# Three row broadcasts: a matmul with a matrix of ones replaced by a write to DRAM and a broadcast read on GpSimd's queue

## The chip, the cores and the metric

The kernel runs on one core of a Trainium2 chip. The metric is device microseconds of one execution of the whole program; the figure given for the kernel before is the median of three runs.

A core has TensorE (PE in the profile, with its weight loads as PEld), VectorE (DVE), ScalarE (ACT), GpSimd (POOL) and SyncE (SP). SP, ACT and POOL also issue DMAs; "SPq", "ACTq" and "POOLq" are these engines as issuers.

## What is computed

One transformer block with adaptive layer norm, batch 1, 2048 tokens, width D = 1024, in bf16:

```python
mod = (silu(c) @ w_mod).reshape(1, 6, 1, 1024)      # c: (1, 1024), w_mod: (1024, 6144)
sa, ca, ga, sb, cb, gb = mod[:, 0], ..., mod[:, 5]
h = layernorm(x) * (1 + ca) + sa
x = x + ga * attention(h)          # 32 query heads on 4 cached kv heads, the last 512 keys, then @ wo
h = layernorm(x) * (1 + cb) + sb
x = x + gb * (silu(h @ w_gate) * (h @ w_up) @ w_down)   # inner width 3584
```

Three vectors of 1024 elements are needed as rows that are the same on all 128 partitions: the gates `ga` and `gb`, which multiply outputs that lie with tokens on the partitions, and `silu(c)`, the conditioning row. That one is multiplied with transposed slices of `w_mod` on VectorE to make the last 24 columns of `mod`.

## The kernel before, in words

All operations are recorded through a tracker, `T.op(stream, emit, reads, writes)` (L80), which puts semaphore waits ahead of an instruction on its engine from the buffers that it reads and writes. Instructions run on each engine in the order in which the program records them; a wait holds all that stands behind it on the same engine. DMAs recorded with a stream of GpSimd are issued by GpSimd in its own instruction order.

The program has an opening (loads, statistics, the first projections), attention on the first 1024 tokens (iterations i = 0 to 65 of `attend`, with `pre0` and `tick0`), the output projection `o_phase(0)`, attention on the second 1024 tokens (i = 64 to 129, with `pre1` and `tick1`), `o_phase(1)`, and the feed-forward part. Large products use a seven-product scheme on 2 x 2 blocks, so sums of weight blocks have to be prepared ahead of their use.

One iteration of `attend` handles one head on 512 tokens: `pre(i)`, part of a query projection, the scores of iteration i - 1 (L797, four matmuls of 512 columns into PSUM banks 0 to 3, then two exponentials on ACT at L805 over two banks each), the products with v for iteration i - 2 (L808: reciprocal at L824, normalisation at L827 on VectorE, and a DMA transpose at L830 on SP), the rest of a query projection, and `tick(i)`. In the first 24 iterations queries are projected whole (`qproj`, copied out of PSUM at L656); later in seven products with sums at L835 and L906.

Beside attention runs the preparation of weight sums for `wo` and `w_down` in units of 512 KB (`unit_chain`, L962). `unit_load` (L945) issues a load on GpSimd's queue into one of two slots, `unit_sums` makes four sums on VectorE (L956) and issues a store on GpSimd's queue (L960). The load for the unit after the next one goes into the slot just stored, so GpSimd waits for the store to land before it issues it.

The conditioning: `silu(c)` lies as `sc_bf`, element k * 128 + p on partition p, column k. The columns of `mod` come out the same way, in `mod_bf`. `ga` is made by matmuls in iterations 12 to 14; the last 24 columns by `mod_col` (L603) on VectorE, one every fourth iteration from i = 19 to 111, each a multiplication of a transposed slice of `w_mod` with `sc_row`, summed along the row. After the last, `mod_take` (L608) copies them to `mod_bf`.

To turn such a [128, 8] block into a row on all partitions, `row_task` (L612) does this: ACT copies the block to f32 (L613); for each of two halves ACT makes four matrices of 128 x 128, each the identity scaled per partition by one column (L618); PE multiplies a matrix of ones with them, which puts the four columns as 512 row elements on every partition in PSUM bank 7 (`XB`); VectorE copies that bank to the row (L626). Matmuls all have line L272 in the profile.

`row_task` is a generator. It is put into the list `bgx` at three places: in `pre0(5)` for `sc_row`, in `pre0(14)` for `rowb[0]` (`ga`), and in `mods(111)` for `rowb[1]` (`gb`). `run_x`, called in `tick0` and `tick1`, moves it on by one step. A row task therefore takes three calls. `rowb[0]` is first read in `o_phase(0)`, `rowb[1]` in the feed-forward part.

GpSimd otherwise does small work: a few fills at the start, among them `ones_bf`, and for each tile of tokens two operations that make the reciprocal standard deviation (L418 and L420 in `aggr`, L535 and L536 in `rstd_of`).

The softmax here doesn't subtract the row's maximum and nothing guards it: scores larger than these inputs give would overflow.

## Time and profile before

| | |
|---|---|
| median of 3 runs | 1160.29 us (1160.15 to 1160.33) |
| profiled execution, time | 1160.09 us |
| profiled execution, span of the core | 1158.3 us |
| granted TensorE clock | full speed throughout |
| PE busy | 1148.3 us |
| DVE busy | 817.4 us |
| ACT busy | 532.7 us |
| POOL busy | 68.4 us |
| DMA | 179.98 MB, 155 GB/s over the span |
| row tasks run at | 45 to 52 us, 78 to 86 us, 500 to 528 us |

How to read it: the span runs from the first to the last instruction of the program; the execution's time is a little longer. In a list of groups, a line gives source line, engine, operation, out<-in by tile names (`arena` is one large SBUF tensor that holds most tiles, `ps` is PSUM), partitions x elements and type, count, then busy time, mean ns of one instruction, and the idle time of the engine just before such instructions with what ended it. In a timeline, a line gives start and length in microseconds, and in brackets the idle time before it and what released it. The chain of waits is followed backwards from the last instruction: at each step to what released it, or to the instruction before it on the same engine. Matmuls are pipelined, so the length of one says less than the distance to the start of the next.

### The profile page before, as it was taken

Reading aid. Unit: us, or ns where it says so; the run is one execution under the profiler, and the core shown is the slowest. Engines: PE = TensorE matmul, PEld = TensorE weight load, DVE = VectorE, ACT = ScalarE, POOL = GpSimd, SP = SyncE. Lnnn points to the kernel's source line nnn. Section 1 sums busy time; section 2 is a strip of 40 time slices with the busy share of each in tenths; the row PEclk is TensorE's granted clock in tenths of the full one; section 3 lists DMA queues with packets and bytes.
Section 4 is the critical chain, followed back from the end, with each engine's and each line's share of the span. In section 5 each row is a group of like instructions: output and inputs, shape, how many; then the busy total and the mean of one; then the engine's idle time right before and its main releaser. Section 6 shows DMA issues by size and latency. Waiting matters only on the chain.

```text
span 1158.3 us, 18250 instructions
## 1 busy us (share of the span) xinstructions
PE 1148.3 (99%) x7105; PEld 588.0 (51%) x7105; DVE 817.4 (71%) x1638; ACT 532.7 (46%) x745; POOL 68.4 (6%) x137
## 2 busy tenths in 40 slices
PE   8999999999999999999999999999999999999999
PEld 5565556654445666656444444444444444444444
DVE  4858897757567777686567898777558777776536
ACT  3867777731127777787110354454110444544110
POOL 1100221100000111111000010000000000000000
PEclk9999999999999999999999999999999999999999
DMA  9679999976807898844875332323774424234443
GB/s 330 145 181 207 225 217 211 236 182 194 242 3 183 197 194 204 203 94 119 191 198 165 87 95 73 108 75 100 209 201 143 121 73 109 73 98 131 130 160 109
DMA packets 289941, 179.98 MB, mean 155 GB/s; under 512 B 130496, under 2 KB 278080, under 8 KB 289856
## 3 DMA queue, kind: packets, MB, share of 16 engines
q1 hardware_dynamic: 226880, 92.31, 35.5%
q10 hardware_dynamic: 54336, 55.05, 15.0%
q0 software_dynamic: 8640, 31.46, 9.3%
q8 instruction: 56, 0.92, 0.3%
q14 instruction: 29, 0.24, 0.1%
HBM read 128.45 MB, written 19.92 MB: 128 GB/s over the span
## 4 chain that ended last, share of the span: by engine, by line
PE 96%; DVE 2%; ACT 1%; DMA 1%; issue 0%; SPq 0%; ACTq 0%; DVEq 0%
PE ps L272 96%; ACT arena L805 1%; DMA arena<-in_A_wq_dram 1%; DVE arena L835 1%; DVE arena L906 0%; DVE st L413 0%; SPq L341 0%; SPq L310 0%; PE ps L276 0%; ACT arena L618 0%; DVE arena L852 0%; ACT tmp L743 0%; DVE arena L1566 0%; ACT L1551 0%; DVE arena L827 0%
## 5 line engine op out<-in xcount | busy, mean ns | idle before, releaser
L272 PE MATMUL ps<-arena 128*128 128x512 f16 (+2 forms) x6800 | 1141.2, 330 | 7.0 <-POOL arena L406 2.2
L272 PEld LDWEIGHTS ps<-arena 128*128 128x128 bf16 (+1 forms) x6800 | 577.8, 98 | 563.0 <-DVE arena L835 6.2
L805 ACT ACTIVATE arena<-ps 128x1024 bf16<-128x1024 f32 x256 | 261.5, 1022 | 44.6 <-PE ps L272 32.8
L838 ACT ACTIVATE tmp<-ps 128x512 f32<-128x512 f32 x167 | 99.7, 597 | 295.9 <-PE ps L272 280.8
L906 DVE TENSOR_TENSOR arena<-arena 128x512 f16<-128x512 bf16 x328 | 133.3, 419 | 3.0
L835 DVE TENSOR_TENSOR arena<-ps,tmp 128x512 bf16<-128x512 f32 (+1 forms) x134 | 91.8, 685 | 49.3 <-PE ps L272 37.8
L838 ACT ACTIVATE nsc<-ps 128x512 f32<-128x512 f32 x84 | 50.1, 596 | 93.2 <-PE ps L272 90.9
L827 DVE TENSOR_TENSOR arena<-ps,rl 128x512 f16<-128x512 f32 x128 | 88.5, 691 | 4.9 <-DVE rl L824 0.5
L835 DVE TENSOR_TENSOR arena<-ps,nsc 128x512 f16<-128x512 f32 x84 | 57.3, 687 | 41.2 <-PE ps L272 30.0
L824 DVE RECIPROCAL rl<-ps 128x4 f32<-128x4 f32 x128 | 23.1, 180 | 87.1 <-PE ps L272 86.2
L1551 ACT ACTIVATE arena<-arena 128x512 f16<-128x512 f16 x84 | 49.9, 624 | 32.4 <-DVE arena L835 32.4
L1122 DVE TENSOR_TENSOR tmp<-ps,tmp 128x512 f32<-128x512 f32 x32 | 22.1, 690 | 58.5 <-ACT tmp L838 48.8
L1046 DVE TENSOR_TENSOR arena<-arena 128x2048 f16<-128x2048 f16 (+3 forms) x56 | 56.0, 1010 | 9.3 <-PE ps L272 8.8
L838 ACT ACTIVATE arena<-ps 128x512 f32<-128x512 f32 x16 | 9.6, 597 | 90.5 <-PE ps L272 90.5
L956 DVE TENSOR_TENSOR arena<-arena 128x512 f16<-128x512 bf16 x120 | 47.9, 419 | 2.0 <-DMA arena<-in_A_wo_dram 0.9
L413 DVE BATCH_NORM_STATS2 st<-x_res 128x6 f32<-128x512 bf16 x58 | 39.5, 682 | 3.7 <-DMA x_res<-in_A_x_dram 3.5
L1566 DVE TENSOR_TENSOR arena<-arena 128x512 f16<-128x512 f16 x84 | 35.0, 416 | 0.3
L1123 DVE TENSOR_TENSOR tmp<-tmp,rowb 128x512 f32<-128x512 f32 (+1 forms) x49 | 33.7, 687 | 1.7
L427 DVE TENSOR_SCALAR nsc<-x_res,mv,rstd 128x1024 f16<-128x1024 bf16 (+1 forms) x30 | 16.2, 539 | 23.3 <-DMA arena<-nsc 22.4
L603 DVE SCALAR_TENSOR_TENSOR arena<-arena 128x1024 bf16<-128x1024 bf16 x24 | 29.2, 1215 | 0.0
L1124 DVE TENSOR_TENSOR arena<-tmp,x_res 128x512 bf16<-128x512 f32 (+1 forms) x33 | 22.3, 676 | 1.1
L835 DVE TENSOR_TENSOR arena<-ps,rowb 128x512 f16<-128x512 f32 x28 | 19.3, 690 | 3.9 <-ACT rowb L838 3.4
(87 smaller groups left out, 333.4 us busy)
## 6 DMA issues: line engine op xcount, KB each, us to landing
arena<-in_A_wq_dram SPq DMA_DIRECT2D x28, 512.0 KB, 5.3
arena<-wo_sum ACTq DMA_DIRECT2D x7, 2048.0 KB, 8.6
arena<-in_B_w_gate_dram SPq DMA_DIRECT2D x28, 512.0 KB, 4.0
arena<-in_B_w_up_dram SPq DMA_DIRECT2D x28, 512.0 KB, 5.1
arena<-wd_sum ACTq DMA_DIRECT2D x8, 1792.0 KB, 7.8
arena<-in_B_w_down_dram ACTq DMA_DIRECT2D x6, 1792.0 KB, 7.1
arena<-in_A_wo_dram POOLq DMA_DIRECT2D x16, 512.0 KB, 4.8
wo_sum<-arena POOLq DMA_DIRECT2D x16, 512.0 KB, 4.6
```

Source lines behind the costliest of these rows:

```text
L272: T.op(PE, lambda: TE.matmul(out_ap, lhsT, rhs, start=start, stop=stop, skip_group_check=skip), reads=reads, writes=[bank_buf])
L413: T.op(DVE, lambda: V.bn_stats(st_[sl][:, hf * 6:hf * 6 + 6], x_res[:, t, hf * 512:hf * 512 + 512]), reads=[B_x[t]], writes=[B_st[sl]])
L805: T.op(ACT, lambda: A.activation(ex_s[es][:, 2 * kp:2 * kp + 2, :], banks2(SCB + 2 * kp), AF.Exp, scale=att_scale), writes=[PB[SCB + 2 * k ...
L827: T.op(DVE, lambda: V.tensor_tensor(o_s[os_].rearrange("p (a b) d -> p a b d", a=2), psap(PVB * 512, [[512, 2], [130, 2], [1, P]]), rlb, A ...
L835: T.op(DVE, lambda: V.tensor_tensor(out, bank(ba), other, ADD), reads=[ob2], writes=[PB[ba], ob])
L838: T.op(ACT, lambda: A.activation(dst, bank(bk), AF.Copy), writes=[PB[bk], db])
L906: T.op(st, lambda: eng.tensor_tensor(o, a, b, op), reads=rd, writes=[wr])
L956: T.op(DVE, lambda: V.tensor_tensor(o, a, b, SUB), reads=rd, writes=[wr])
L1046: T.op(DVE, lambda: V.tensor_tensor(o, a, b, SUB), reads=rd, writes=[sb])
L1123: T.op(DVE, lambda: V.tensor_tensor(tm, tm, rw, MULT), reads=[B_row[row]], writes=[tb])
L1551: T.op(ACT, lambda: A.activation(o, s_, AF.Silu), reads=[sb], writes=[ob])
L1566: T.op(DVE, lambda: V.tensor_tensor(gu[blk][:, p, :], o, s_, MULT), reads=[sb, ob], writes=[B_gu[blk][p]])
```

## The change

`row_task`, its buffers (`c6`, `ones_bf`, the four `diag` matrices), the list `bgx` and all calls of `run_x` go. In their place `row_of` issues two DMAs from GpSimd's queue at the three places where a row task had been put into the list: the first writes the [128, 8] block into a DRAM tensor of 1024 elements in row order, the second, which waits for the first to land, reads that row to all 128 partitions with a step of zero.

```diff
-            T.op(POOL, lambda: g.memset(ones_bf, 1.0), writes=[B_ones])
...
-            def row_task(dst, dbuf, src, sbuf):
-                T.op(ACT, lambda: A.activation(c6[:, :], src, AF.Copy), reads=[sbuf], writes=[B_c6])
...
-                for n in range(2):
-                    for q in range(4):
-                        mm(bank(XB, P, q * P), ones_bf, diag[q], q == 0, q == 3, [B_ones, B_diag[q]], PB[XB], skip=True)
-                    T.op(DVE, lambda: V.tensor_copy(dst[:, n * 512:(n + 1) * 512], bank(XB)),
-                         writes=[PB[XB], dbuf])
-                    if n == 0:
-                        diags(1)
-                    yield
+            Q_row = [[dq("q_row%d_%d" % (n, m), nc.gpsimd) for m in range(2)] for n in range(3)]
+            rows_d = [nc.dram_tensor("row%d" % n, [D], BF16).ap() for n in range(3)]
+
+            def row_of(n, dst, dbuf, src, sbuf):
+                b_ = _Buf("rowd%d" % n)
+                T.op(Q_row[n][0], lambda: g.dma_start(rows_d[n].rearrange("(k p) -> p k", p=P), src, allow_slow_non_contiguous=True), reads=[sbuf], writes=[b_])
+                every = bass.AP(tensor=rows_d[n].tensor, offset=0, ap=[[0, P], [1, D]])
+                T.op(Q_row[n][1], lambda: g.dma_start(dst, every), reads=[b_], writes=[dbuf])
...
-                            bgx.append(row_task(rowb[1], B_row[1], mod_bf[:, 5 * DT:6 * DT], B_late[3]))
+                            row_of(1, rowb[1][:, :], B_row[1], mod_bf[:, 5 * DT:6 * DT], B_late[3])
...
-                    bgx.append(row_task(sc_row, B_scr, sc_bf[:, :], B_sc))
+                    row_of(2, sc_row, B_scr, sc_bf[:, :], B_sc)
...
-                        bgx.append(row_task(rowb[0], B_row[0], mod_bf[:, NE:NF], B_late[0]))
+                        row_of(0, rowb[0][:, :], B_row[0], mod_bf[:, NE:NF], B_late[0])
...
-                if i < 20 or i % 4 == 0:
-                    run_x()
```

## The prediction

> **What bounds the kernel now.** I read the busy shares first, then the chain that ended last, then the PE waits, and only then the surroundings of the three row tasks. The page:

> ```profile
> PE 1148.3 (99%) x7105; PEld 588.0 (51%) x7105; DVE 817.4 (71%) x1638; ACT 532.7 (46%) x745; POOL 68.4 (6%) x137
> PE 96%; DVE 2%; ACT 1%; DMA 1%; issue 0%; SPq 0%; ACTq 0%; DVEq 0%
> ```

> TensorE is the bound: it is busy 99% of the span and holds 96% of the chain. So a matmul removed is worth its streaming time, and ACT, VectorE or GpSimd work is worth something only where PE waits for it. After the first 16 us the list of waits has few entries (waited for, total, times, longest):

> ```profile
> PE ps L272 <- ACT arena L805: 1.4, 4, 0.5
> PE ps L272 <- DVE arena L835: 1.1, 3, 0.4
> PE ps L272 <- DVE arena L432: 0.5, 1, 0.5
> ```

> L805 is the exponential. The chain restricted to 40 to 120 us shows that some of its 1.4 us belong to the first row task (start, length, engine, tile, line):

> ```profile
> 44.14 1.02 ACT arena L805
> 45.16 0.11 ACT c L613
> 45.27 0.02 issue
> 45.29 1.28 ACT arena L618 x4
> 46.57 0.92 ACT arena L805
> ...
> 48.65 5.25 PE ps L272 x50
> ```

> L613 and L618 are the row task's scaled-identity copies. They stand between two exponentials on ACT, and PE stands behind the second. From the starts of single matmuls in the trace, PE's next score matmul starts at 47.53, 0.41 us later than back to back, and the third at 48.65, 0.67 us later. The copies of the second and third row (78 to 83 us; 500 and 514 us) are followed by no PE gap.

> The row matmuls themselves, by form (count, busy, mean ns, idle before):

> ```profile
> L272 PE MATMUL ps<-arena 128*128 128x128 bf16 x24 | 2.3, 219 | 0.0
> ```

> 219 ns is a pipelined duration; what one costs PE is the distance between starts, 56 ns in the trace.

> [...]here it makes 1024 writes of 2 bytes per row, 64 on each of 16 engines. [...] The trace shows such waits on this queue, 3.55 us for a store below.

> **Part by part.** All times are against the profiled execution, 1160.09 us (span 1158.3 and 1.8 around it), 0.20 under the median 1160.29.

> *PE work removed.* 24 matmuls x 56 ns = 1.34 us. Second row: 8 x 56 = 0.45 us, PE being gapless there. Third row: 0.45 likewise.

> *First row (sc_row), PE and ACT together.* Without the copies the exponential waits only for PE's two score matmuls, which end near 45.75 instead of ACT starting at 46.48. Two halves of 1.06 follow, so PE's third score matmul can start at 47.93 instead of 48.65: 0.72 gained (the first four row matmuls lay inside that stall). The four later ones add 4 x 56 = 0.22. Sum 0.94. The later stall behind L432 stays: VectorE was idle 0.33 us for PE just before it, so both move together.

> *VectorE.* Six PSUM copies of 0.68 us go (4.1 us). In none of their places does PE wait for VectorE in the next microseconds, so I count nothing. If the cover were gone it would be a gain, at most the 1.1 + 0.5 us above.

> *GpSimd memset of the ones.* 0.20 us at 1.42 us; PE's start is later held by weights landing (0.85 us idle at 11.58). Nothing; bounds 0 and -0.2.

> Gross gain 0.94 + 0.45 + 0.45 = 1.84 us.

> *What is added: six DMAs in GpSimd's order.* GpSimd issues the write, waits for its landing, issues the broadcast read; everything behind it in program order waits too. The consumers of the rows are far away: sc_row is first multiplied at 94 us, the gate rows after 260 us. So only the queue behind counts.

> First row (sc_row), near 44 us: GpSimd is then idle 11.09 us, until two unit loads at 55.13. Free up to some 9 us of write. Its packets share engines with the last norm transposes (landing 48.15), needed at 51.62, nearer 50.1 once VectorE is relieved; 0 to 1 us, I take 0.

> Third row, 497 us: behind it wait a pair of rstd operations (499.15, no reader for tens of microseconds) and the last store (501.73). Free.

> Second row, 76 us, is where it matters. GpSimd around it:

> ```profile
> 79.61 0.71 POOL L945 DMA_DIRECT2D arena<-in_A_wo_dram  x1 [3.55 <-DMA wo_sum<-arena]
> 87.20 0.57 POOL L960 DMA_DIRECT2D wo_sum<-arena  x1 [6.87 <-DVE arena L956]
> 92.53 0.71 POOL L945 DMA_DIRECT2D arena<-in_A_wo_dram  x1 [4.76 <-DMA wo_sum<-arena]
> ```

> The write is issued at 80.32, right behind a 512 KB load on the same queue; that load lands at 87.37. The queue works in order: two loads issued 0.95 us apart at 55.13 land 3.6 us apart. So the write lands at 87.37 + w. Size of w: the profile's queue table gives 35.5% x 16 x 1158.3 / 226880 = 29 ns per packet of 407 B and 51 ns per packet of 1013 B, which extrapolates to 14 ns at no size, 64 x 14 = 0.9 us. [...] I take 30 ns: w = 1.9, landing 89.3. Issuing the read (0.7) moves the store from 87.20 to 90.0. The store landed 4.8 after issue; the 256 KB read ahead of it adds 128 packets / 16 x 0.09 = 0.7. So the load of 92.53 goes out at 95.5, three late. It landed at 98.07 and was first read at 100.09, 2.0 us of slack; with PE 0.45 further ahead VectorE then waits 3.0 + 0.45 - 2.0 = 1.45 us. What VectorE has to give:

> ```profile
> 100.09 0.88 DVE L956 TENSOR_TENSOR arena<-arena 128x512 f16<-128x512 bf16 x2
> 101.34 0.18 DVE L824 RECIPROCAL rl<-ps 128x4 f32<-128x4 f32 x1 [0.37 <-PE ps L272]
> ...
> 103.97 0.18 DVE L824 RECIPROCAL rl<-ps 128x4 f32<-128x4 f32 x1 [0.26 <-PE ps L272]
> ```

> 0.37 + 0.26 = 0.63 us of idleness, then it runs solid until PE already waits for it at 110.7. So PE loses 1.45 - 0.63 = 0.8 us. Each further microsecond of w is a further microsecond lost.

> The issue of 1024 descriptors on GpSimd itself: the 0.57 of a store with 128 rows against 0.71 of a load with 256 source rows gives about 1 ns per descriptor, 1.5 us in all, hidden behind the load that is still moving. At three times that it would still end before 87.37.

> Sum: 1160.09 - 1.84 + 0.8 = 1159.05; on the scale of the median 1159.3.

> **Rivals**, on the median's scale.

> *Clean saving.* w near 0.9 and a load that catches up (between 92 and 95 us it had waited for other traffic): loss 0, gain 1.84, 1158.4. For it: the load issued at 92.53 took 5.5 us. Against: the same traffic meets the store.

> *GpSimd's queue becomes the bound (slower).* Price: the write of the second row, place: the unit load read at 100.09. The loss equals the gain at w = 1.9 + 1.04 = 2.9 us (46 ns per element); it is slower by over 0.2% (2.3 us, about what a measurement of this kernel can tell from no change) from a loss of 4.16, w = 5.3 (82 ns per element). At 150 ns: w = 9.6, loss 0.8 + 7.7 = 8.5, 1166.9. For it: 16 engines write bytes of the same 2 KB[...]. Against: the 14 ns that the smallest packets suggest.

> *More waits vanish.* ACT is relieved of 3 x (0.20 + 2 x 1.28) = 8.3 us and VectorE of 4.1; if all later waits behind L835 and L432 went too, 1158.4 - 1.6 = 1156.8. Against: they recur where no row task is near.

> *The change doesn't do what it says.* The broadcast might be confined to few engines, 256 KB then taking several microseconds ahead of the store: on one engine 128 x 0.09 = 11.5 instead of 0.7, a loss of 11.6 and 1170. Against: both sides of the read count 128 on their outer dimension, as the existing loads do. It is counted with the queue rival.

> **Numbers.** Net gain of 0 to 1.84 us (my forecast and the clean saving) 0.45; net loss under 2.3 us 0.15; queue rival 0.33; more waits vanish 0.07. So same 0.60, slower 0.33, faster 0.07. The forecast's own range is 1158.4 to 1160.3. The range from 1157.8 to 1167 leaves out some 0.04 below and 0.14 above.

> **What would show it.** The 24 matmuls of 128x128 gone; no PE gap between 45 and 50 us, except the one behind the exponential; PE about 0.9 us ahead at 55 us and 1.4 ahead at 90; the store of 87.20 at about 89 to 90; VectorE waiting for a DMA of in_A_wo_dram at L956 near 100 us, and PE behind L835 by 0.8 us more near 110; nothing new near 500 us. Wrong, if GpSimd waits more than 10 us for a row's write, if the unit loads at 55 us move, or if the store does not move at all.

## The result, and the profile after

The changed kernel takes **1190.37 us** (median of 6 runs, 1188.0 to 1195.07) against 1160.24 us for the kernel before in the same comparison (6 runs, 1160.02 to 1160.33): a ratio of 1.0266, 95% interval 1.0245 to 1.0286. The forecast was 1159.3 us with a range from 1157.8 to 1167; it was wrong by 31 us. The profiled execution of the changed kernel took 1188.0 us, its span is 1186.2 us, 27.9 more than before. Line numbers have moved: L268 is the matmul (L272 before), L789 the exponential (L805), L811 the normalisation (L827), L640 the cast out of PSUM (L656), L427 the modulation (L432), L814 the transposes on SP (L830), L929, L940 and L944 the unit load, sums and store (L945, L956, L960). L612 is the new write, L614 the new read.

The page after, busy time of the engines and the chain that ended last:

```profile
PE 1148.6 (97%) x6995; PEld 588.6 (50%) x7081; DVE 814.0 (69%) x1632; ACT 525.9 (44%) x718; POOL 73.4 (6%) x142
PE 91%; DMA 3%; issue 2%; DVE 1%; ACT 1%; SPq 0%; POOL 0%; ACTq 0%; DVEq 0%; POOLq 0%
```

TensorE's share of the chain fell from 96% to 91%, and DMAs and "issue" took it. TensorE is busy for as long as before although the row matmuls are gone (a few of its records are missing as well), so some matmuls became longer. GpSimd's timeline around the three rows (start, length, and in brackets the idle time before and its releaser):

```profile
43.74 1.13 POOL L612 DMA_DIRECT2D row<-sc_bf  x1
59.21 0.59 POOL L614 DMA_DIRECT2D arena<-row  x1 [14.34 <-DMA row<-sc_bf]
62.56 1.44 POOL L929 DMA_DIRECT2D arena<-in_A_wo_dram  x2 [2.76 <-DVE arena L811]
...
89.77 0.93 POOL L612 DMA_DIRECT2D row<-mod_bf  x1
109.34 0.56 POOL L614 DMA_DIRECT2D rowb<-row  x1 [18.64 <-issue]
109.90 0.56 POOL L944 DMA_DIRECT2D wo_sum<-arena  x1
118.39 0.71 POOL L929 DMA_DIRECT2D arena<-in_A_wo_dram  x1 [7.93 <-DMA wo_sum<-arena]
...
523.01 0.90 POOL L612 DMA_DIRECT2D row<-mod_bf  x1 [8.68 <-DVE rl L808]
538.34 0.57 POOL L614 DMA_DIRECT2D rowb<-row  x1 [14.43 <-DMA row<-mod_bf]
```

Issuing 1024 elements costs GpSimd about 1 us. The landing of 2 KB takes 14.3 and 14.4 us where the queue is otherwise empty. In the second row the wait is 18.6 us; the profile names no releaser there ("issue"), but by the program it is the wait for the same kind of write, behind a unit load that lands at 94.31, 15.0 us before it ends. Beside that stand the waits of TensorE (total, times, longest):

```profile
PE ps L268 <- DVE arena L640: 16.0, 2, 8.8
PE ps L268 <- DVE arena L811: 5.6, 1, 5.6
```

Neither was in the list before. The chain restricted to 40 to 135 us tells what VectorE was late for:

```profile
44.45 14.96 DMA arena<-nsc
...
61.50 3.59 PE ps L268 x8
...
90.70 18.64 issue
109.34 0.55 POOL rowb L614
109.90 7.93 DMA wo_sum<-arena
...
118.39 6.28 DMA arena<-in_A_wo_dram
```

The pieces from 90.70 on are the mechanism of the forecast: GpSimd's wait for the row's write, then the store and the load behind it. The first piece, 14.96 us for a transpose of `nsc` (normalised tokens) from SBUF to SBUF, has nothing to do with GpSimd's queue: SP issued it. The eight matmuls after it start 427 ns apart, twice the usual 216. The granted clock is half after each of TensorE's three long gaps (8.8, 7.2 and 5.6 us), until 65.1, 116.3 and 130.0 us, and 0.988 on average instead of 1.0.

What the DMA engines do while the second row's write is in flight, in the stretch from 98 to 108 us (busy tenths in 40 slices, then packets), after:

```profile
DMA  0019992990000000090000000000000000000100
DMA packets 520, 0.15 MB, mean 15 GB/s; under 512 B 505, under 2 KB 519, under 8 KB 519
q8 instruction: 1, 0.02, 5.2%
```

and before, in the same stretch of time:

```profile
DMA  9799699899999945998799999999993761244269
DMA packets 2882, 2.52 MB, mean 252 GB/s; under 512 B 1181, under 2 KB 2205, under 8 KB 2882
```

Nearly nothing moves for seven of these ten microseconds, although SP has a 512 KB load and a transpose outstanding. The one packet of the instruction queue takes 5.2% x 16 x 10 = 8.3 us, where such packets take 0.9 to 1.6 us in the kernel before. It is not alone: packets of 4 to 512 bytes of the transposes and loads that start beside it take up to 8.9 us, where no packet in this stretch of the kernel before takes more than 3.2. VectorE and ACT stop and start again together, and the profile gives "remote" as the releaser, in a program of one core: nothing that it knows. VectorE's timeline:

```profile
59.44 1.41 DVE L427 TENSOR_SCALAR arena<-arena,gain,mod_bf 128x512 f16<-128x512 f16 x4 [9.27 <-DMA arena<-nsc]
...
109.93 0.69 DVE L640 CAST arena<-ps 128x512 bf16<-128x512 f32 x1 [8.31 <-remote]
...
124.70 0.88 DVE L940 TENSOR_TENSOR arena<-arena 128x512 f16<-128x512 bf16 x2 [6.32 <-DMA arena<-in_A_wo_dram]
```

and ACT's:

```profile
109.99 2.14 ACT L789 ACTIVATE arena<-ps 128x1024 bf16<-128x1024 f32 x2 [9.15 <-remote]
```

That their instructions came late because the fetch of instructions stood in the same jam fits the packet of 8.3 us. The trace's records of semaphores offer another reading. Both instructions wait for TensorE. No semaphore changes between 99.85 and 109.40 us in these records, although TensorE starts 27 more matmuls by 103.28; their updates then come from 109.80 on, some 33 ns apart, closer together than the matmuls themselves. So TensorE's reports of finished matmuls were late as well, or only their records were. Both readings are inferences, no run isolates either.

Both traces hold all 256 exponentials of attention. Matched one by one, their starts tell how far the changed kernel is behind, in microseconds (negative: ahead); the stretches are given in the times of the kernel before:

| stretch of the kernel before | behind at its start | at its end | added |
|---|---|---|---|
| 43 to 58 us, first row | -0.25 | 8.55 | 8.8 |
| 73 to 107 us, second row | 8.55 | 25.28 | 16.7 |
| 498 to 529 us, third row | 25.39 | 27.57 | 2.2 |

The sum is 27.7 of the 27.9 measured. The forecast's gain is inside these figures: in the first stretch the changed kernel first gets 0.92 us further ahead, in the second it first makes up 0.45. So the writes cost 9.7 us in the first row and 17.2 in the second, and with the forecast's 0.45 some 2.5 in the third. These three places hold nearly the whole loss. Two causes compete for it: GpSimd's queue is **held** by the wait for the write, or the write **clogs** the DMA engines for everyone.

### The profile page after: what moved, and what is told of

Its sections match the earlier page's. It is cut to its first block, busy times and chain, and to the rows that moved or that the text cites. A ratio compares the mean times of both kernels' runs of the same rounds, so it can differ in the third digit from the quotient of the medians.

```text
span 1186.2 us, 18088 instructions
## 1 busy us (share of the span) xinstructions
PE 1148.6 (97%) x6995; PEld 588.6 (50%) x7081; DVE 814.0 (69%) x1632; ACT 525.9 (44%) x718; POOL 73.4 (6%) x142
## 3 DMA queue, kind: packets, MB, share of 16 engines
q1 hardware_dynamic: 226880, 92.31, 37.2%
q10 hardware_dynamic: 54336, 55.05, 14.3%
## 4 chain that ended last, share of the span: by engine, by line
PE 91%; DMA 3%; issue 2%; DVE 1%; ACT 1%; SPq 0%; POOL 0%; ACTq 0%; DVEq 0%; POOLq 0%
PE ps L268 91%; DMA arena<-nsc 1%; DMA wo_sum<-arena 1%; ACT arena L789 1%; DVE arena L819 1%; DMA arena<-in_A_wq_dram 1%; DMA arena<-in_A_wo_dram 1%; SPq L336 0%; SPq L305 0%; PE ps L272 0%; DVE arena L811 0%; DVE arena L890 0%; DVE arena L836 0%; DVE arena L940 0%; ACT tmp L727 0%
## 5 line engine op out<-in xcount | busy, mean ns | idle before, releaser
L268 PE MATMUL ps<-arena 128*128 128x512 f16 (+2 forms) x6690 | 1141.1, 331 | 34.7 <-DVE arena L640 16.0
L268 PEld LDWEIGHTS ps<-arena 128*128 128x128 bf16 (+1 forms) x6776 | 578.4, 98 | 591.0 <-DVE arena L640 16.6
L789 ACT ACTIVATE arena<-ps 128x1024 bf16<-128x1024 f32 x256 | 261.5, 1022 | 72.5 <-PE ps L268 51.7
L811 DVE TENSOR_TENSOR arena<-ps,rl 128x512 f16<-128x512 f32 x128 | 88.5, 691 | 5.3 <-DMA arena<-arena 0.9
L822 ACT ACTIVATE nsc<-ps 128x512 f32<-128x512 f32 x84 | 50.1, 596 | 93.2 <-PE ps L268 90.9
L940 DVE TENSOR_TENSOR arena<-arena 128x512 f16<-128x512 bf16 x120 | 47.8, 419 | 7.3 <-DMA arena<-in_A_wo_dram 6.3
L427 DVE TENSOR_SCALAR arena<-arena,gain,mod_bf 128x512 f16<-128x512 f16 x56 | 20.4, 409 | 9.3 <-DMA arena<-nsc 9.3
```

The lines of the kernel that those rows point to most:

```text
L268: T.op(PE, lambda: TE.matmul(out_ap, lhsT, rhs, start=start, stop=stop, skip_group_check=skip), reads=reads, writes=[bank_buf])
L789: T.op(ACT, lambda: A.activation(ex_s[es][:, 2 * kp:2 * kp + 2, :], banks2(SCB + 2 * kp), AF.Exp, scale=att_scale), writes=[PB[SCB + 2 * k ...
L811: T.op(DVE, lambda: V.tensor_tensor(o_s[os_].rearrange("p (a b) d -> p a b d", a=2), psap(PVB * 512, [[512, 2], [130, 2], [1, P]]), rlb, A ...
L822: T.op(ACT, lambda: A.activation(dst, bank(bk), AF.Copy), writes=[PB[bk], db])
L940: T.op(DVE, lambda: V.tensor_tensor(o, a, b, SUB), reads=rd, writes=[wr])
```

## The experiments

**The read alone.** The element writes go, the reads take `c` from its input (other values, the same 256 KB).

```diff
-                T.op(Q_row[n][0], lambda: g.dma_start(rows_d[n].rearrange("(k p) -> p k", p=P), src, allow_slow_non_contiguous=True), reads=[sbuf], writes=[b_])
-                every = bass.AP(tensor=rows_d[n].tensor, offset=0, ap=[[0, P], [1, D]])
+                every = bass.AP(tensor=c.tensor, offset=0, ap=[[0, P], [1, D]])
```

> The changed kernel without its three element writes: each broadcast read takes the 1024 elements of the input c instead, so the row values are left out. Clog theory (while 1024 two-byte writes to DRAM are under way, about 14 us, no other transfer gets on, and PE waits for those others): without the writes nothing is left of the loss, 1158.4 us (the gross gain of 1.84 us against before), range 1157.5 to 1159.5. Queue theory (GpSimd waits for the landing and what stands behind it in its order is late): the same 1158.4. If it is above 1162, the loss lies in the broadcast reads or in something that the removal of the row tasks set free.

Measured: 1159.65 us (12 runs) against 1160.66 (15 runs), ratio 0.9993 (0.9984 to 1.0001). The broadcast reads cost nothing that shows, and the whole loss goes with the writes. Measured from just ahead of the first row, where this run happens to be 0.38 us behind, TensorE is 0.91 us ahead of the kernel before at 53 us and 1.24 at 98.

**The write on ACT's queue, GpSimd never waiting for it.** ACT issues the write, GpSimd the read 6, 10 and 11 iterations later, to come after the landing.

```diff
-            Q_row = [[dq("q_row%d_%d" % (n, m), nc.gpsimd) for m in range(2)] for n in range(3)]
+            Q_row = [[dq("q_row%d_%d" % (n, m), nc.gpsimd if m else nc.scalar) for m in range(2)] for n in range(3)]
...
+                if i in (11, 24, 122):
+                    row_get({11: 2, 24: 0, 122: 1}[i])
```

> The same element writes at the same places, but issued by ACT on its own DMA queue, and the broadcast reads issued by GpSimd 6, 10 and 11 iterations later, when the write has long landed: GpSimd never waits for a write and nothing of its queue stands behind one. Clog theory: the loss stays, 1175 to 1195 us, the DMA engines nearly idle for about 14 us after each write, and PE waiting for the norm transposes near 50 us. Queue theory: the loss goes, 1158 to 1161 us.

Measured: 1196.78 us (4 runs), ratio 1.0314 (1.0296 to 1.0331): no better than the changed kernel, and just above the range of the clog theory. TensorE's waits and then, from the chain, the two long pieces by the first and second row:

```profile
PE ps L268 <- DVE arena L817: 13.2, 1, 13.2
PE ps L268 <- DVE arena L646: 11.6, 1, 11.6
```

```profile
40.85 17.26 DMA arena<-nsc
...
97.35 17.69 DMA arena<-in_A_wo_dram
```

A transpose on SP and a unit load on GpSimd, both issued without waiting for the row, each take over 17 us behind ACT's write. The first write lands at 57.95 us, just before the transpose; the landing of the second is not in the trace, but the DMA engines move little from 94 to 105 us, and GpSimd's queue moves nothing from 94 to 111. The clog does it, and it needs no held queue.

**The queue held without the clog.** Six writes of 8 x 256 B, each waiting for the one before, in place of the element write (the row is `c`, not the block).

```diff
-                T.op(Q_row[n][0], lambda: g.dma_start(rows_d[n].rearrange("(k p) -> p k", p=P), src, allow_slow_non_contiguous=True), reads=[sbuf], writes=[b_])
+                for _ in range(6):
+                    T.op(Q_row[n][0], lambda: g.dma_start(rows_d[n].rearrange("(k p) -> k p", p=P), c_row[:, :]), reads=[sbuf, B_cT], writes=[b_])
```

> The changed kernel with each element write replaced by six writes of 8 rows of 256 B (taken from the untreated c, so the row values are left out), each of which waits for the landing of the one before[...]. Clog theory: first and third row cost nothing; the store of the second row moves from 87 to about 94 to 95 us and VectorE waits some 5 us for a unit load near 105 us: 1163 us, range 1159 to 1167. Queue theory: as the changed kernel, 1185 to 1195.

Measured: 1179.5 us (4 runs, 1176.4 in the profiled one), ratio 1.0157 (1.0141 to 1.0174), between the ranges of the two theories. The hold lasted longer than planned, some 24 us in the second row, because each of the six waits takes 1.3 to 6.2 us there; the store goes out at 105.07 instead of the expected 94 to 95. GpSimd and TensorE's wait there:

```profile
79.56 0.71 POOL L930 DMA_DIRECT2D arena<-in_A_wo_dram  x1 [4.54 <-DMA wo_sum<-arena]
...
105.07 0.55 POOL L945 DMA_DIRECT2D wo_sum<-arena  x1
110.26 0.72 POOL L930 DMA_DIRECT2D arena<-in_A_wo_dram  x1 [4.64 <-DMA wo_sum<-arena]
```

```profile
PE ps L268 <- DVE arena L812: 15.1, 1, 15.1
```

The load in the second row is issued 17.7 us later than the 92.53 of the kernel before (the load ahead of it, at 79.56 and 79.61, puts both on one scale). The forecast's formula gives TensorE a loss of 17.7 + 0.45 - 2.0 - 0.63 = 15.5 us; the gap is 15.1. The first and third rows, held 20 and 14 us, cost nothing: TensorE's gaps there equal those of the read alone. So holding the queue matters in the second row only, as forecast, and there it would be nearly enough by itself: in the changed kernel the load is 118.39 - 92.53 - 9.47 (the whole program is that much behind, 89.08 against 79.61) = 16.4 us late, and the formula gives 14.2 of the 17.2 lost. Hold and clog overlap there and don't add.

**Half the elements.** Only the first four columns are written, 512 elements into 1 KB, read twice into each row.

```diff
-                T.op(Q_row[n][0], lambda: g.dma_start(rows_d[n].rearrange("(k p) -> p k", p=P), src, allow_slow_non_contiguous=True), reads=[sbuf], writes=[b_])
-                every = bass.AP(tensor=rows_d[n].tensor, offset=0, ap=[[0, P], [1, D]])
+                T.op(Q_row[n][0], lambda: g.dma_start(rows_d[n][0:D // 2].rearrange("(k p) -> p k", p=P), src[:, 0:DT // 2], allow_slow_non_contiguous=True), reads=[sbuf], writes=[b_])
+                every = bass.AP(tensor=rows_d[n].tensor, offset=0, ap=[[0, P], [0, 2], [1, D // 2]])
```

> The changed kernel with only the first 512 elements of each row written (one element per descriptor as before) and read twice; the other half of each row is left out. Clog theory: each write lasts about 7 us instead of 14, GpSimd's waits for it fall to about 7 to 9 us, and the loss to about a third or half of 30: 1168 to 1178 us. Queue theory, with the prediction's own sum: second row only, 0.8 + (7.7 - 1.9) = 6.6 lost, 1165 us, and nothing near 50 us.

Measured: 1198.58 us (4 runs), ratio 1.032 (1.0305 to 1.0336). GpSimd's timeline, the three reads:

```profile
63.03 0.74 POOL L614 DMA_DIRECT2D arena<-row  x1 [18.17 <-DMA row<-sc_bf]
...
116.14 0.71 POOL L614 DMA_DIRECT2D rowb<-row  x1 [20.13 <-DMA row<-mod_bf]
...
547.60 0.71 POOL L614 DMA_DIRECT2D rowb<-row  x1 [17.18 <-DMA row<-mod_bf]
```

Half the elements take no less than all of them. The landing is not a price per element, which both theories had assumed, and the forecast too. What the two kernels share is density: 32 elements of two bytes to each 64 bytes of DRAM. The next runs vary that.

**A step of 8 bytes, 128 bytes, 32 bytes.** The same 1024 elements, spread in DRAM; the rows are read from `c` in all three. The edit for 8 bytes (`[DT, P, 4]`; 64 and 16 in the last place for 128 and 32 bytes):

```diff
-            rows_d = [nc.dram_tensor("row%d" % n, [D], BF16).ap() for n in range(3)]
+            rows_d = [nc.dram_tensor("row%d" % n, [DT, P, 4], BF16).ap() for n in range(3)]
...
-                T.op(Q_row[n][0], lambda: g.dma_start(rows_d[n].rearrange("(k p) -> p k", p=P), src, allow_slow_non_contiguous=True), reads=[sbuf], writes=[b_])
+                T.op(Q_row[n][0], lambda: g.dma_start(rows_d[n].rearrange("k p e -> p k e")[:, :, 0], src, allow_slow_non_contiguous=True), reads=[sbuf], writes=[b_])
```

> The changed kernel, writing the same 1024 two-byte elements with a step of 8 bytes in DRAM (so 8 KB instead of 2 KB); the broadcast reads take the input c instead, so the row values are left out, but still wait for the write. Collision theory (elements that fall into the same stretch of 64 bytes are written one after the other, by several engines, some 0.45 to 0.6 us each: 32 x 0.45 = 14 us, and half the elements take as long because the density is the same): 8 per 64 bytes, GpSimd's wait for the write falls to 4 to 6 us and the time to 1161 to 1168 us. Count theory (the cost is per descriptor, or fixed per such DMA): waits of 14 to 18 us as before, 1185 to 1200 us.

> As e_stride8 with a step of 128 bytes, so no two elements share 64 bytes (the row values are left out likewise). Collision theory: the wait for the write falls to 2 to 4 us beyond other traffic, no idle stretch of the DMA engines, and the time to 1158 to 1162 us. Count theory: 14 to 18 us and 1185 to 1200 us.

> The element write with a step of 32 bytes (1024 elements over 32 KB, 2 to each 64-byte stretch; rows read from c, values not those of the reference). Between the step of 8 bytes (5.1 and 4.7 us) and that of 128 (3.1 and 3.1). If the time goes by the number of elements that share 64 bytes, the first and third wait are 3.2 to 3.7 us;[...] if elements that share 32 bytes or less are what collides, no more than 3.1. Time 1160 to 1164 in each case, the second row losing little.

Measured: 8 bytes 1168.0 us (4 runs), ratio 1.0069 (1.005 to 1.0087); 128 bytes 1163.52 (19 runs from 1158.86 to 1170.06; the profiled one 1159.54 with no new wait), ratio 1.0021 (1.0003 to 1.0039); 32 bytes 1160.53 (20 runs), ratio 1.0 (0.999 to 1.0011). GpSimd's timeline at a step of 8 bytes, then of 128, then of 32:

```profile
50.24 0.58 POOL L614 DMA_DIRECT2D arena<-in_c_dram  x1 [5.10 <-DMA row<-sc_bf]
...
510.52 0.57 POOL L614 DMA_DIRECT2D rowb<-in_c_dram  x1 [4.68 <-DMA row<-mod_bf]
```

```profile
48.68 0.59 POOL L614 DMA_DIRECT2D arena<-in_c_dram  x1 [3.12 <-DMA row<-sc_bf]
...
500.94 0.57 POOL L614 DMA_DIRECT2D rowb<-in_c_dram  x1 [3.14 <-DMA row<-mod_bf]
```

```profile
49.94 0.59 POOL L614 DMA_DIRECT2D arena<-in_c_dram  x1 [3.15 <-DMA row<-sc_bf]
...
504.35 0.57 POOL L614 DMA_DIRECT2D rowb<-in_c_dram  x1 [3.32 <-DMA row<-mod_bf]
```

The same number of elements and bytes: 14.3 us at 2 bytes, about 5 at 8, 3.1 to 3.3 at 32 and 128. Closeness of the elements is the cause. The median at 128 bytes lies above the expected 1158 to 1162 us. The cases of the last expectation lie too near each other for 3.15 and 3.32 to decide; the size of the stretch within which closeness counts stays open, and the 64 bytes of the expectations are an assumption of the author. At 8 bytes the second row alone loses: TensorE waits 6.6 us. The load there is issued at 98.52, 5.8 us late on the scale of the kernel before, which by the formula is 3.6, and takes 8.1 us to land instead of 5.5: together 6.2. Why the single times at 128 bytes scatter by 11 us is open; in the ten slower runs, and in no other, the mean granted clock is below 1 (0.996 to 0.999), but none of them left a trace.

**Runs of 16 bytes.** The write goes to place 8p + k, so that a partition's eight elements lie together (the row is permuted).

```diff
-                T.op(Q_row[n][0], lambda: g.dma_start(rows_d[n].rearrange("(k p) -> p k", p=P), src, allow_slow_non_contiguous=True), reads=[sbuf], writes=[b_])
+                T.op(Q_row[n][0], lambda: g.dma_start(rows_d[n].rearrange("(p k) -> p k", p=P), src), reads=[sbuf], writes=[b_])
```

> The changed kernel with the rows written in partition order, 128 runs of 16 bytes instead of 1024 of 2, same 2 KB; the rows then hold their elements in another order, which is left so. Collision theory: 4 runs per 64 bytes, some 2 us more than a plain small write: waits of 3 to 5 us, 1159 to 1164 us. Count theory: 128 descriptors of 14 ns are 1.8 us: the same. If the cost came with the bytes written (2 KB): 14 us and 1185 or more.

Measured: 1160.2 us (12 runs), ratio 0.9996 (0.9987 to 1.0004); GpSimd waits 2.62 and 1.43 us in the first and third row, less than the expected 3 to 5. The same 2 KB in 128 pieces, still four pieces to 64 bytes, cost next to nothing: it is not the bytes.

**Neighbours from one partition.** The destination of the last run, but written element by element from a strided source, so that neighbouring elements come from one partition.

```diff
-                T.op(Q_row[n][0], lambda: g.dma_start(rows_d[n].rearrange("(k p) -> p k", p=P), src, allow_slow_non_contiguous=True), reads=[sbuf], writes=[b_])
+                T.op(Q_row[n][0], lambda: g.dma_start(rows_d[n].rearrange("(p k) -> p k", p=P), x_res[:, 0, 0:2 * DT:2], allow_slow_non_contiguous=True), reads=[sbuf, B_x[0]], writes=[b_])
```

> The source is replaced by every second element of a token tile, 8 of them from each partition, and the element of partition p and column k goes to place 8p + k instead of 128k + p; the rows are read from c, so their values are not those of the reference. Still 1024 elements of two bytes, 32 to each 64-byte stretch of the same 2 KB, but a partition's 8 elements now lie side by side[...]. Theory one, writes into the same stretch follow one another whoever issues them: GpSimd waits 14 to 18 us for each row as in the changed kernel, time 1186 to 1195. Theory two, only writes of different engines into the same stretch collide: 3 to 5 us at the first and third row, nothing lost there, time 1160 to 1168.

Measured: 1202.77 us (4 runs), ratio 1.0363 (1.0328 to 1.0399), the slowest of all. GpSimd's timeline:

```profile
66.10 0.58 POOL L614 DMA_DIRECT2D arena<-in_c_dram  x1 [20.91 <-DMA row<-x_res]
...
124.00 0.57 POOL L614 DMA_DIRECT2D rowb<-in_c_dram  x1 [25.58 <-DMA row<-x_res]
...
559.68 0.56 POOL L614 DMA_DIRECT2D rowb<-in_c_dram  x1 [19.14 <-DMA row<-x_res]
```

19 to 26 us: longer than in the changed kernel, and above the expected 14 to 18. Taking eight neighbours in a row from one partition makes the landing no shorter. No view shows which engine writes which place; that different engines meet in a stretch in the changed kernel and not here was an assumption of the author. If it holds, a meeting of different engines is not needed, and of the two theories the first is left, that writes into the same stretch follow one another whoever issues them; that they take 19 to 26 us here and 14.3 in the changed kernel, at the same closeness, it doesn't explain.

**A version without element writes.** One transpose on TensorE turns the block into [8, 128], VectorE copies it to SBUF, GpSimd writes eight runs of 256 B, and the reads are issued iterations later (i = 7, 24, 116), to come after the landing. For the two gates the block is turned at i = 15 and 112.

```diff
-                T.op(Q_row[n][0], lambda: g.dma_start(rows_d[n].rearrange("(k p) -> p k", p=P), src, allow_slow_non_contiguous=True), reads=[sbuf], writes=[b_])
+                T.op(PE, lambda: TE.transpose(bank_bf(XB)[0:DT, 0:P], src, ident), reads=[sbuf, B_ident], writes=[PB[XB]])
+                T.op(DVE, lambda: V.tensor_copy(row8[n], bank_bf(XB)[0:DT, 0:P]), writes=[PB[XB], B_row8[n]])
+                T.op(Q_row[n][0], lambda: g.dma_start(rows_d[n].rearrange("(k p) -> k p", p=P), row8[n]), reads=[B_row8[n]], writes=[b_])
+                later[n] = (dst, dbuf, b_)
```

> Meant to be better than both: the [128, 8] block is turned by one PE transpose into 8 rows of 128, VectorE copies them to SBUF, GpSimd writes 8 runs of 256 bytes, and issues the broadcast read 2, 9 and 4 iterations later, in stretches where it is idle. PE: 24 x 56 ns less, 3 x 56 more, and the wait behind the ACT copies gone (0.45): 1.6 us saved against before, ratio 0.9986. Nothing in its GpSimd waits over 1 us for a row. Queue theory: the same. If the small writes of 256 bytes clogged the engines like those of 2 bytes: 1175 or more.

Measured: 1159.49 us (13 runs, 1158.91 to 1160.82) against 1160.47 (40 runs), ratio 0.9991 (0.9982 to 0.9999). It is 31 us faster than the changed kernel and 1.0 us faster than the kernel before, of 1.6 expected; that interval only just leaves out no change. GpSimd's timeline at the first row:

```profile
46.72 0.74 POOL L616 DMA_DIRECT2D row<-arena  x1 [1.01 <-DVE rl L818]
50.05 0.58 POOL L624 DMA_DIRECT2D arena<-row  x1 [2.59 <-DMA row<-arena]
```

The wait of 2.59 us is a miss of the expectation (none over 1 us), harmless because GpSimd is idle there anyway.

## Why the prediction was wrong, point by point

*The size of w, the term that was mis-sized.* "I take 30 ns: w = 1.9", with 150 ns and 9.6 us at the upper end, an assumption of the author that no trace showed. Measured by the undisturbed first and third row, the landing took 14.3 and 14.4 us, and in the second row it came 15.0 us after that of the load ahead of it: outside both ends. Its form was wrong too, 64 elements on each of 16 engines times a price (the trace of the changed kernel has such a write as 16 packets of 128 B): 1024 elements on a step of 128 bytes take 3.1 us, 512 packed densely 17 to 18. The packets from which the price was drawn have 407 and 1013 bytes on average, and none belongs to a transfer that scatters elements. The upper end had the same form, a price for each piece, side by side on 16 engines. If writes into one stretch go one after another, an estimate from these runs with 64 bytes as the stretch is (14.3 - 3.1) / 31 = 0.36 us for each further write, (5.1 - 3.1) / 7 = 0.29 at 8 bytes and 0.5 to 0.6 in the half kernel and in the one with neighbours from one partition: of one order, not one number. That the time goes by how close the pieces lie is what the series shows; that they wait for each other fits it and is not shown. The 0.7 us for the read (128 packets at 0.09 us) was an estimate too; 0.09 us lies on the line through the same two averages, at 2 KB. In the changed kernel a read goes as 64 packets of 4 KB and lands 3.8 to 7.0 us after its issue.

*"Its packets share engines with the last norm transposes ... 0 to 1 us, I take 0."* This is the second step that failed: 9.7 us in the first row. The forecast asked how much the 2 KB would take of the engines' time. The loss is that other transfers stand still or crawl until the small writes are done: 14.96 us for the transpose of `nsc`, over 17 in the kernel with ACT's queue.

*"Third row ... Free."* Free for the queue, as the held-queue run confirms; but the transposes on SP crawl there too (10.1 us to the landing, against 2.4 to 4.3 between 495 and 530 us in the kernel before), and TensorE loses 2.5 us.

*The second row.* The mechanism was right, with its place and its formula: store late, load late, VectorE waits at the unit sums, TensorE behind it; 15.5 worked out and 15.1 measured where only the queue was held. With the true w the same sum gives most of the loss. Not foreseen were the stall of VectorE and ACT themselves (8.3 and 9.2 us) and the half clock after the gaps (4.6 us, an estimate: half of the 5.6 and 3.5 us that TensorE works in it).

*The gross gain of 1.84.* Its parts are confirmed by the exponentials: 0.92 us in the first row of the changed kernel and 0.91 with the read alone (forecast 0.94), 0.45 in the second row of both. The forecast's 47.93 for the third score matmul can't be read off, because that matmul has no record in the changed kernel's trace; the one that starts at 47.93 is the fourth. At the end 1.0 us is left, by the read alone and by the transposed version; both intervals reach to 1.84. In the profile of the read alone 1.1 us of the lead go between 150 and 343 us: TensorE waits there three times for VectorE and ACT, 1.4 us in all, and the kernel before has no such wait in that stretch.

*The rivals.* "GpSimd's queue becomes the bound" had the right sign and a fifth of the size: at its end of 150 ns it gave 1166.9, 6.6 us above the kernel before instead of 30. The read was not confined to few engines; it costs nothing that shows. Of the conditions named for "wrong", two came about: a wait of more than 10 us for a row's write, and the unit loads of 55 us moved to 62.56 (there behind VectorE, which waited for the transpose, and not behind the row's read).

## What to carry to other kernels

A DMA that scatters two-byte elements into neighbouring places of DRAM must not be priced by its bytes or its number of pieces (2 KB took 14.3 us as 1024 neighbouring elements and 1.4 to 2.6 as runs of 16 bytes; 1024 elements on a step of 32 or 128 bytes took 3.1 to 3.3): ask how many pieces fall close together, and expect that other transfers, on other queues too, stand behind it (here a transpose on SP's queue, 15.0 us instead of 3.1 to 3.4). Turn the block on chip first, so that DRAM gets runs of 256 B (here one small transpose and one copy per row; GpSimd then waited 2.6 us in the first row), and issue the read back late enough that the queue does not wait for the landing. Where a DMA's form is not in the trace, an upper bound from other forms is no bound; leave the range open on that side.
